# Layer norm, attention and SwiGLU on one core: row 0's mean from two scaled sums, its statistics behind row 1's

## The chip, the cores and the metric

The kernel runs on one core of one Trainium2 chip. The metric is the device time of one execution in microseconds; the time given is the median of several. Lower is better.

## The reference

```python
def reference(A_x, A_wqkv, A_wo, B_x, B_w_gate, B_w_up, B_w_down):
    x  = A_x                                  # 1 x 2048 x 576, bf16
    xn = _layernorm(x)                        # (x - mean) / sqrt(var + 1e-5)
    # A: 32 heads of 18, each token sees itself and 7 tokens at steps of 2 behind it
    q, k, v = split(xn @ wqkv)
    logits = q . k[pos - 2*w] * 18**-0.5, w = 0..7   # masked to -1e9 where pos - 2*w < 0
    o = softmax(logits) . v[pos - 2*w]
    # B: SwiGLU with 4608 hidden columns
    return x + o @ wo + (silu(xn @ w_gate) * (xn @ w_up)) @ w_down
```

Bodies are shortened here; all inputs are bf16 and drawn as normal values times 0.05.

## The kernel before

The 2048 tokens are cut into 16 rows of 128 tokens: partition p holds tokens 16p to 16p+15, and row r is the r-th token of every partition. A row's work is then 128 partitions by 576 columns. The kernel runs in two stages.

**QKV stage, the first 60 us.** Rows of x are loaded (row 0 through ACT's queue, rows 1 to 3 one by one and the rest in three blocks of four through SP's). For each row DVE takes the statistics (`ln_stats`: `bn_stats` on each half of the columns in `ln_half`, then `bn_aggr` in `ln_aggr`), ACT the square root of the variance (`ln_sqrt`), DVE its reciprocal (`ln_recip`) and the normalized row (`ln_apply`). The normalized row is 576 columns and a copy of its last 64, 640 in all, so that the contraction makes four slabs (kt) of 128 and a fifth, kt=4, of twice the same 64. The row is transposed into `xnT`: rows 1 to 4 on TensorE (`transp_pe` for row 1, `transp_halves` for rows 2 to 4, with copies out of PSUM by ACT and DVE), rows 5 and on by a transposing DMA (`transp_dma`). Then TensorE multiplies it with wqkv in four groups g of 432 columns (`p_mm`, L301), and `p_evac` takes the sums out of PSUM.

Row 0 differs. Its QKV product is taken from the centered row alone: `ln_center` (L251) subtracts the mean, `ln_center_pad` does it for the last 64 columns on GpSimd, TensorE transposes it, the copies go to `xcT` instead of `xnT`, and `p_evac(0, ...)` multiplies with 1/std while it takes the sums out (L365, L367). Since the second stage wants the normalized row 0 in `xnT` too, `ln_apply(0)` makes it in `xn0` (in the space of the later tile A) and `transp_dma(0)` turns it.

Row 0 multiplies with whole 128-row slabs for kt 0 to 3 (`p_whole`). Its kt=4 (`p_row0_rest`) and all of the later rows use two 64-row halves that run beside each other (`p_row`). Where the two halves exchange their banks a GpSimd no-op stands between them as a fence (`fence_after`, `fence_before`, L314): the matmul behind it waits for GpSimd's queue to come to that point.

PSUM has 8 buffers, taken in turn: the warm-up's (also `pt1`), `pa` and `pb` for transposes, `t` for row 0's four groups, `u` for row 1's.

**The second stage** runs over four blocks of 512 tokens. For each it multiplies `xnT` with w_gate and w_up (L600), takes silu and the product (L611 to L613), and multiplies the result with w_down and the attention's output with wo (L629). The attention itself is DVE work that is interleaved there (`chain`).

The order of the work is written out by hand: `manual_schedule` keeps each engine's instructions in the order of the calls. Every engine runs its queue in that order, so the calls on lines 477 to 550 are the order on each engine. SP's queue issues nearly all transfers, and a transfer that waits for its data holds up those behind it. The start, before:

```python
    warm_pe(10, 1)
    ln_open(0)
    ln_stats(0)
    ln_center_pad(0)
    ln_center(0, 0, P)
    ln_sqrt(0)
```

The functions that the diff touches, and what calls them:

Of the kernel before, what the change touches and what calls it, by code (L numbers as in the profile page):

```python
# [10 lines left out]
f32 = mybir.dt.float32  # L11
ACT = mybir.ActivationFunctionType
ALU = mybir.AluOpType
# [4 lines left out]
P = 128  # L18
H, DH, W, DIL = 32, 18, 8, 2
D = H * DH  # L20
HALF = D // 2
# [4 lines left out]
DPAD = KT * P  # L26
# [44 lines left out]
def kernel(  # L71
# [11 lines left out]
    nc = tc.nc  # L83
# [9 lines left out]
    const = ctx.enter_context(tc.tile_pool(name="const", bufs=1))  # L93
# [19 lines left out]
    PP = big.tile([P, 2, RT * D], bf16, name="PP")  # L113
# [65 lines left out]
    def load_gu(it):  # L179
        ch, slot = it % NCH, it % NSLOT  # L180
        fc = slice(ch * FC * P, (ch + 1) * FC * P)
        nc.sync.dma_start(gu[:, slot, 0:4, :], B_w_gate[0:512, fc].rearrange("(kt kp) n -> kp kt n", kp=P))
        nc.sync.dma_start(gu[:, slot, 4:8, :], B_w_up[0:512, fc].rearrange("(kt kp) n -> kp kt n", kp=P))
        nc.sync.dma_start(gu[0:64, slot, 8, :], B_w_gate[512:576, fc])
        nc.sync.dma_start(gu[64:128, slot, 8, :], B_w_up[512:576, fc])
# [10 lines left out]
    def new_ps(name):  # L196
        return ps.tile([P, 512], f32, name=name, tag="ps")


    ln = {}  # L200

    def ln_open(c):
        mv = lns.tile([P, 4, 2], f32, name="mv")
        rstd = lns.tile([P, 4], f32, name="rstd")
        ln[c] = (xc_b[c], xn_b[c % 2], mv, rstd)

    sums = {}

    def ln_half(r, k):
        c, j = divmod(r, 4)  # L210
        xc, xn, mv, rstd = ln[c]
        if k == 0:
            sums[r] = lns.tile([P, 2, 6], f32, name="stats")
        nc.vector.bn_stats(sums[r][:, k, :], xc[:, j, k * HALF:(k + 1) * HALF])  # L214

    def ln_aggr(r):
        c, j = divmod(r, 4)
        nc.vector.bn_aggr(ln[c][2][:, j, :], sums[r][:].rearrange("p c s -> p (c s)"))

    def ln_stats(r, n=1):  # L220
        for i in range(r, r + n):
            ln_half(i, 0)
            ln_half(i, 1)
            ln_aggr(i)

    def ln_sqrt(r, n=1):
        c, j = divmod(r, 4)
        xc, xn, mv, rstd = ln[c]
        nc.scalar.activation(rstd[:, j:j + n], mv[:, j:j + n, 1], ACT.Sqrt, bias=eps_t[:], scale=1.0)

    def ln_recip(r, n=1):
        c, j = divmod(r, 4)
        rstd = ln[c][3]
        nc.vector.reciprocal(rstd[:, j:j + n], rstd[:, j:j + n])

    def ln_apply(r):
        c, j = divmod(r, 4)
        xc, xn, mv, rstd = ln[c]
        dst = xn[:, j] if r else xn0
        nc.vector.tensor_scalar(dst[:, 0:D], xc[:, j], mv[:, j, 0:1], rstd[:, j:j + 1],  # L240
                                op0=ALU.subtract, op1=ALU.mult)
        if r < 2:
            nc.gpsimd.tensor_scalar(dst[:, D:DPAD], xc[:, j, 512:D], mv[:, j, 0:1], rstd[:, j:j + 1],
                                    op0=ALU.subtract, op1=ALU.mult)
        else:
            nc.vector.tensor_copy(dst[:, D:DPAD], dst[:, 512:D])

    def ln_center(r, lo=0, hi=D):
        c, j = divmod(r, 4)
        xc, xn, mv, rstd = ln[c]  # L250
        nc.vector.tensor_scalar(xn[:, j, lo:hi], xc[:, j, lo:hi], mv[:, j, 0:1], None, op0=ALU.subtract)  # L251

    def ln_center_pad(r):
        c, j = divmod(r, 4)
        xc, xn, mv, rstd = ln[c]
        nc.gpsimd.tensor_scalar(xn[:, j, D:DPAD], xc[:, j, 512:D], mv[:, j, 0:1], None, op0=ALU.subtract)

    def transp_pe(r, kts, pt):
        c, j = divmod(r, 4)
        xn = ln[c][1]  # L260
        for i, kt in enumerate(kts):
            nc.tensor.transpose(pt[:, i * P:(i + 1) * P], xn[:, j, kt * P:(kt + 1) * P], ident[:])  # L262

    def xT_of(r):
        return xcT if r == 0 else xnT[:, :, r * P:(r + 1) * P]

    def copy_pt(eng, r, kts, pt):
        eng(xT_of(r)[:, kts[0]:kts[-1] + 1, :],
            pt[:, 0:len(kts) * P].rearrange("p (k t) -> p k t", t=P))

    def new_pt():
        return ps.tile([P, 8 * P], bf16, name="pt", tag="ps")
# [16 lines left out]
    def transp_dma(r):  # L289
        c, j = divmod(r, 4)  # L290
        nc.sync.dma_start_transpose(xnT[:, :, r * P:(r + 1) * P], ln[c][1][:, j, :] if r else xn0)
# [7 lines left out]
    def p_mm(t, g, kt, half, r, start, stop):  # L299
        rows = slice(0, P) if half is None else slice(64 * half, 64 * half + 64)  # L300
        return nc.tensor.matmul(t[g][:, 0:G], xT_of(r)[rows, kt, :], w_at(g, kt, rows),  # L301
                                start=start, stop=stop)

    def p_whole(r, t, kt, gs=range(NG)):
        for g in gs:
            p_mm(t, g, kt, None, r, kt == 0, False)
# [14 lines left out]
    def p_row(r, between=None, at=(0, 1), t=None):  # L321


        done = t is not None
        t = t or [None] * NG
        fence = {}
        for swap in range(2):
            for i in range(2):
                for kt in (0, 1, 2, 3) if swap else (0, 4, 1, 2, 3):
                    if done and kt == 0:  # L330
                        continue
                    for half in range(2):
                        g = i + 2 * (half ^ swap)
                        if t[g] is None:
                            t[g] = new_ps("qkv_ps")
                        mm = p_mm(t, g, kt, half, r, swap == 0 and kt == 0, swap == 1 and kt == 3)
                        if swap == 0 and kt == 3 and half == 1:
                            fence[i] = fence_after(mm)
                        if swap and kt == (1 if done else 0) and half == 0:
                            fence_before(mm, fence[i])  # L340
                    if swap and (i, kt) == at and between is not None:
                        between()
        return t

    def p_evac(r, t, only=range(6), between=None, last=6, dve=(5,)):


        c, j = divmod(r, 4)
        ks, vs = stage[2 * c % 4], stage[(2 * c + 1) % 4]
        vdst = vs[:, j, :].rearrange("p (d h) -> p d h", h=H)  # L350
        parts = [
            (QO[:, r, 0:G], t[0][:, 0:G]),
            (ks[:, j, HALF:D], t[2][:, 0:HALF]),
            (vdst[:, :, 0:8], t[2][:, HALF:G].rearrange("p (h d) -> p d h", d=DH)),
            (QO[:, r, G:D], t[1][:, 0:D - G]),
            (ks[:, j, 0:HALF], t[1][:, D - G:G]),
            (vdst[:, :, 8:H], t[3][:, 0:G].rearrange("p (h d) -> p d h", d=DH)),
        ]
        for n in only:
            if n == last:  # L360
                between()
            if r:
                (nc.vector.tensor_copy if n in dve else nc.scalar.copy)(*parts[n])  # L363
            elif n in dve:
                nc.vector.tensor_scalar(*parts[n], ln[0][3][:, 0:1], None, op0=ALU.mult)  # L365
            else:
                nc.scalar.mul(*parts[n], ln[0][3][:, 0:1])  # L367
# [99 lines left out]
    def normalize(r, n=1):  # L467
        ln_recip(r, n)
        for i in range(r, r + n):
            ln_apply(i)  # L470
            if i > 4:
                transp_dma(i)
# [3 lines left out]

    warm_pe(10, 1)
    ln_open(0)
    ln_stats(0)
    ln_center_pad(0)  # L480
    ln_center(0, 0, P)
    ln_sqrt(0)
    pa, pb = new_pt(), new_pt()
    transp_pe(0, (0,), pa)
    ln_center(0, P, D)
# [3 lines left out]
    ln_stats(1)  # L489
    ln_sqrt(1)  # L490
    copy_pt(nc.scalar.copy, 0, (3, 4), pb[:, 2 * P:])
    ln_recip(0)
    ln_apply(0)
    ln_recip(1)
    ln_apply(1)

    t = [new_ps("qkv_ps") for g in range(NG)]
    p_whole(0, t, 0)
    p_whole(0, t, 1)
    p_whole(0, t, 2, (0, 1))  # L500
    transp_pe(1, (0, 1), pt1)
    transp_pe(1, (2,), pa)
    copy_pt(nc.scalar.copy, 1, (0, 1), pt1)
    copy_pt(nc.vector.tensor_copy, 1, (2,), pa)
    p_whole(0, t, 2, (2, 3))
    transp_pe(1, (3, 4), pb)
    copy_pt(nc.scalar.copy, 1, (3, 4), pb)
    u = [None] * NG
    for g in (0, 2, 1, 3):
        u[g] = new_ps("qkv_ps")  # L510
# [2 lines left out]
    p_row0_rest(t)  # L513
    ln_stats(2)
    ln_sqrt(2)
    normalize(2)
    p_evac(0, t, (5, 0, 3, 2, 4, 1), dve=(5, 2))
    ln_half(3, 0)
    ln_half(3, 1)
    load_gu(0)  # L520
    transp_dma(0)

    p_row(1, turn(2), (0, 1), u)
    ln_aggr(3)
# [3 lines left out]
    normalize(3)  # L528
    ln_open(1)
    ln_stats(4)  # L530
    for ring in (Kr, Vr):
        nc.sync.dma_start(ring[0:1, 0:HALO, :], wz[0:1, :].unsqueeze(1).to_broadcast([1, HALO, D]))

    t = p_row(2, turn(3))
    ln_stats(5)
# [5 lines left out]
    t = p_row(3, turn(4))  # L541
# [10 lines left out]
    for r in range(4, R):  # L552
        t = p_row(r)
# [92 lines left out]
    for tt in range(NTT):  # L646
# [28 lines left out]
        for sub in range(0, RT, 2):  # L675
            t, fence = {}, {}
# [36 lines left out]
```

## Time and profile before

| | |
|---|---|
| median of 3 runs | 503.44 us (503.23 to 503.55) |
| the profiled execution | 503.32 us, of which the span of the profile is 501.5 |
| TensorE matmuls | 496.8 us busy, 99% of the span |
| VectorE (DVE) | 329.0 us, 66% |
| ScalarE (ACT) | 200.6 us, 40% |
| GpSimd (POOL) | 2.6 us, 1% |
| row 0 of x landed, first BN_STATS | 3.78 us |
| first QKV matmul | 6.01 us |
| first matmul of the second stage | 59.66 us |

In the profile each row of a time line gives the start in us, the duration, the engine, the line of the kernel and the operation with what it writes and reads; in brackets stand the idle time of the engine just before it and what ended it. PEld is TensorE's weight load, which overlaps the matmuls before it. ACTq and SPq are the sequencers that issue transfers. Matmul ends are modelled, so it is their starts that are compared. A chain line gives start, duration and what the end of the kernel was waiting on in that time.

### The profile page before, as it was taken

How to read it: one execution, taken by the hardware profiler on the slowest of the kernel's cores; microseconds unless marked ns; L12 is line 12 of the kernel's file. 1: busy time of each engine (PE TensorE's matmuls, PEld its weight loads, DVE VectorE, ACT ScalarE, POOL GpSimd, SP SyncE). 2: the span in 40 equal slices, each digit the busy share in tenths (PEclk: the TensorE clock that was granted, in tenths of full speed). 3: DMA queues.
4: the chain of work that ended last, by engine and by line, in shares of the span. 5: the costliest groups of instructions: out<-in, count | busy, mean ns of one | idle time of the engine just before them, and what ended most of it. 6: DMA issues, size and time to landing. Idle time of an engine off the chain costs nothing.

```text
span 501.5 us, 13267 instructions
## 1 busy us (share of the span) xinstructions
PE 496.8 (99%) x5795; PEld 282.8 (56%) x5795; DVE 329.0 (66%) x478; ACT 200.6 (40%) x415; POOL 2.6 (1%) x9
## 2 busy tenths in 40 slices
PE   8999999999999999999999999999999999999997
PEld 4555544444677644444777544445777444446775
DVE  5889597998999698999897139995980222221001
ACT  4756657645300255544300445557000454553000
POOL 2000000000000000000000000000000000000000
PEclk9999999999999999999999999999999999999999
DMA  8689989898731045535631154453700335442200
GB/s 322 164 207 228 320 268 294 260 318 272 186 114 61 25 147 185 190 112 174 166 106 47 30 182 154 131 189 110 181 26 14 106 110 177 159 126 39 76 14 25
DMA packets 77186, 75.42 MB, mean 150 GB/s; under 512 B 22708, under 2 KB 72528, under 8 KB 77128
## 3 DMA queue, kind: packets, MB, share of 16 engines
q1 hardware_dynamic: 76840, 73.98, 49.2%
q8 instruction: 45, 0.74, 0.7%
q10 hardware_dynamic: 288, 0.59, 0.3%
q14 instruction: 13, 0.11, 0.1%
HBM read 58.76 MB, written 5.90 MB: 129 GB/s over the span
## 4 chain that ended last, share of the span: by engine, by line
PE 98%; DMA 1%; DVE 0%; SPq 0%; issue 0%
PE g_ps L600 56%; PE d_ps L629 32%; PE qkv_ps L301 11%; DMA hT<-in_A_wqkv_dram 1%; DVE ot L643 0%; PE pt L283 0%; SPq L145 0%; PE pt L262 0%; PE warm_ps L262 0%
## 5 line engine op out<-in xcount | busy, mean ns | idle before, releaser
L600 PE MATMUL g_ps<-xnT,gu 64*128 64x512 bf16 x2592 | 280.4, 376 | 0.0
L600 PEld LDWEIGHTS <-gu 64*128 64x128 bf16 x2592 | 126.1, 94 | 152.9
L611 ACT ACTIVATE sg<-g_ps 128x512 bf16<-128x512 f32 x144 | 87.3, 606 | 156.6 <-PE g_ps L600 156.6
L629 PE MATMUL d_ps<-wd,hT 64*128 64x288 bf16 x2304 | 146.4, 283 | 0.0
L629 PEld LDWEIGHTS <-hT 64*128 64x128 bf16 x2304 | 112.2, 94 | 29.7
L613 DVE TENSOR_TENSOR hT<-sg,uc 128x512 bf16<-128x512 bf16 x144 | 60.0, 419 | 93.9 <-ACT uc L612 93.8
L612 ACT CAST uc<-g_ps 128x512 bf16<-128x512 f32 x144 | 85.2, 592 | 0.0
L414 DVE TENSOR_REDUCE PP<-PP 128x64 f32<-128x1152 bf16 x64 | 84.9, 1346 | 0.4
L301 PE MATMUL qkv_ps<-hT,xnT 64*128 64x432 bf16 (+1 forms) x536 | 50.1, 343 | 0.0
L409 DVE TENSOR_TENSOR PP<-QO,Kr 128x2304 bf16<-128x2304 bf16 (+1 forms) x35 | 43.5, 1249 | 7.0 <-DMA Kr<-hT 6.8
L641 DVE TENSOR_TENSOR ot<-d_ps,xr 128x288 bf16<-128x288 f32 x30 | 12.3, 450 | 51.1 <-PE d_ps L629 51.1
L441 DVE TENSOR_TENSOR PP<-Vr,A 128x2304 bf16<-128x2304 bf16 (+1 forms) x35 | 43.2, 1250 | 0.4
L301 PEld LDWEIGHTS <-xnT 64*128 64x128 bf16 (+1 forms) x536 | 25.9, 94 | 22.5 <-ACT xnT L287 0.2
L446 DVE TENSOR_TENSOR PP<-PP 128x2304 bf16<-128x2304 bf16 x24 | 32.5, 1353 | 0.3
L611 ACT ACT_TABLE_LOAD x5 | 6.4, 1283 | 47.2 <-PE g_ps L600 47.2
L629 PE MATMUL d_ps<-wo,xnT 64*128 64x288 bf16 x288 | 22.9, 283 | 0.0
L363 ACT CAST hT<-qkv_ps 128x288 bf16<-128x288 f32 (+2 forms) x58 | 21.1, 427 | 0.5 <-ACT hT L363 0.5
L434 ACT ACTIVATE PP<-PP 128x1024 f32<-128x1024 f32 x4 | 4.2, 1056 | 31.2 <-DVE PP L430 31.2
L629 PEld LDWEIGHTS <-xnT 64*128 64x128 bf16 x288 | 14.0, 94 | 3.6
L643 ACT CAST ot<-d_ps 128x288 bf16<-128x288 f32 x1 | 0.4, 399 | 38.8 <-PE d_ps L629 38.8
L363 ACT CAST QO<-qkv_ps 128x432 bf16<-128x432 f32 (+1 forms) x30 | 12.3, 409 | 7.4 <-PE qkv_ps L301 7.4
L214 DVE BATCH_NORM_STATS2 stats<-wd 128x6 f32<-128x288 bf16 x32 | 12.9, 444 | 2.8 <-DMA wd<-in_A_x_dram 2.6
(53 smaller groups left out, 89.4 us busy)
## 6 DMA issues: line engine op xcount, KB each, us to landing
gu<-in_B_w_gate_dram SPq DMA_DIRECT2D x36, 512.0 KB, 3.9
gu<-in_B_w_up_dram SPq DMA_DIRECT2D x36, 512.0 KB, 5.2
wd<-in_B_w_down_dram SPq DMA_DIRECT2D x9, 576.0 KB, 6.4
kv_d<-hT SPq DMA_DIRECT2D x5, 576.0 KB, 6.0
gu<-in_B_w_gate_dram SPq DMA_DIRECT2D x36, 64.0 KB, 5.0
gu<-in_B_w_up_dram SPq DMA_DIRECT2D x36, 64.0 KB, 4.6
xr<-in_A_x_dram SPq DMA_DIRECT2D x8, 288.0 KB, 3.9
out_dram<-ot SPq DMA_DIRECT2D x16, 144.0 KB, 1.8
```

The lines of the kernel that those rows point to most:

```text
L214: nc.vector.bn_stats(sums[r][:, k, :], xc[:, j, k * HALF:(k + 1) * HALF])
L301: return nc.tensor.matmul(t[g][:, 0:G], xT_of(r)[rows, kt, :], w_at(g, kt, rows), start=start, stop=stop)
L363: (nc.vector.tensor_copy if n in dve else nc.scalar.copy)(*parts[n])
L409: nc.vector.tensor_tensor(prod[:, a:b], QO[:, RT * tt + a:RT * tt + b, :], Kr[:, s:s + b - a, :], op=ALU.mult)
L414: nc.vector.tensor_reduce(L[:, w, rs], prod[:, rs].rearrange("p r (h d) -> p r h d", d=DH), axis=AX.X, op=ALU.add)
L441: nc.vector.tensor_tensor(dst[:, a:b], Vr[:, s:s + b - a, :].rearrange("p r (d h) -> p r d h", h=H), A[:, w, a:b].unsqueeze(2).to_broadcas ...
L446: nc.vector.tensor_tensor(dst, acc, pv, op=ALU.add)
L600: mm = nc.tensor.matmul(ring_ps[j][b][:], gu[rows, slot, k, fc], xnT[rows, kt, tok], start=(swap == 0 and kt == 0), stop=(swap == 1 and kt ...
L611: nc.scalar.activation(sg[:], t[0][:], ACT.Silu)
L612: nc.scalar.copy(uc[:], t[1][:])
L613: nc.vector.tensor_tensor(hT[:, ch * FC + j, :], sg[:], uc[:], op=ALU.mult)
L629: mm = nc.tensor.matmul(t[sub][h][:, 0:HALF], a[rows], w[rows, h * HALF:(h + 1) * HALF], start=(swap == 0 and n == 0), stop=(swap == 1 and ...
```

## The change

Row 0's mean no longer comes from `bn_stats` and `bn_aggr`. A new function `ln_mean0` sums each half of the columns, scaled by 1/576: the first half by an ACT activation with an accumulator output, the second by a DVE tensor_scalar with one. The two parts stand in a new tile `part`, and `ln_center` and `ln_center_pad` subtract both in one instruction (the diff of the pad, on GpSimd, is the same as that of `ln_center`). The scaled elements themselves go to a part of PP that nothing reads.

Row 0's statistics are still needed for 1/std. They are taken behind row 1's: the first half while row 1 waits for its square root, the second half and the aggregate behind row 1's normalization. Row 0's square root comes behind row 1's copies out of PSUM, its reciprocal behind row 2's statistics. Row 1's transposes stand one matmul earlier among row 0's kt=2 groups, and the copy of its third block goes from DVE to ACT. `ln_apply(0)` goes behind row 4's statistics, and `transp_dma(0)` behind the two writes of the halo's zeros on SP.

```diff
+    part = const.tile([P, 2], f32, name="part")
+    def ln_mean0():
+        xc = ln[0][0]
+        nc.scalar.activation(PP[:, 1, 0:HALF], xc[:, 0, 0:HALF], ACT.Copy, scale=1.0 / D, accum_out=part[:, 0:1])
+        nc.vector.tensor_scalar(PP[:, 1, HALF:D], xc[:, 0, HALF:D], 1.0 / D, None,
+                                op0=ALU.mult, op1=ALU.add, accum_out=part[:, 1:2])
...
     def ln_center(r, lo=0, hi=D):
...
-        nc.vector.tensor_scalar(xn[:, j, lo:hi], xc[:, j, lo:hi], mv[:, j, 0:1], None, op0=ALU.subtract)
+        nc.vector.tensor_scalar(xn[:, j, lo:hi], xc[:, j, lo:hi], part[:, 0:1], part[:, 1:2],
+                                op0=ALU.subtract, op1=ALU.subtract)
...
     ln_open(0)
-    ln_stats(0)
+    ln_mean0()
     ln_center_pad(0)
     ln_center(0, 0, P)
-    ln_sqrt(0)
     pa, pb = new_pt(), new_pt()
...
     ln_stats(1)
     ln_sqrt(1)
     copy_pt(nc.scalar.copy, 0, (3, 4), pb[:, 2 * P:])
-    ln_recip(0)
-    ln_apply(0)
+    ln_half(0, 0)
     ln_recip(1)
     ln_apply(1)
+    ln_half(0, 1)
+    ln_aggr(0)
...
     p_whole(0, t, 1)
-    p_whole(0, t, 2, (0, 1))
+    p_whole(0, t, 2, (0,))
     transp_pe(1, (0, 1), pt1)
     transp_pe(1, (2,), pa)
     copy_pt(nc.scalar.copy, 1, (0, 1), pt1)
-    copy_pt(nc.vector.tensor_copy, 1, (2,), pa)
-    p_whole(0, t, 2, (2, 3))
+    p_whole(0, t, 2, (1, 2))
     transp_pe(1, (3, 4), pb)
+    copy_pt(nc.scalar.copy, 1, (2,), pa)
     copy_pt(nc.scalar.copy, 1, (3, 4), pb)
+    p_whole(0, t, 2, (3,))
+    ln_sqrt(0)
...
     ln_stats(2)
     ln_sqrt(2)
+    ln_recip(0)
     normalize(2)
...
     load_gu(0)
-    transp_dma(0)
...
     ln_stats(4)
+    ln_apply(0)
     for ring in (Kr, Vr):
         nc.sync.dma_start(ring[0:1, 0:HALO, :], wz[0:1, :].unsqueeze(1).to_broadcast([1, HALO, D]))
+    transp_dma(0)
```

More of the change, by code (lines that the diff above doesn't have):

```diff
@@ L255, in ln_center_pad @@
         xc, xn, mv, rstd = ln[c]
-        nc.gpsimd.tensor_scalar(xn[:, j, D:DPAD], xc[:, j, 512:D], mv[:, j, 0:1], None, op0=ALU.subtract)
+        nc.gpsimd.tensor_scalar(xn[:, j, D:DPAD], xc[:, j, 512:D], part[:, 0:1], part[:, 1:2],
+                                op0=ALU.subtract, op1=ALU.subtract)
     def transp_pe(r, kts, pt):
```

## The prediction

> **What bounds the kernel now.** I read the share of each engine first, then the chain that ended last over the first 15 us, then the time line of the start, and last the single rows of TensorE (starts to the nanosecond, rounded here to 0.01 or 0.001 us).
>
> The page and the chain:
> ```profile
> PE 496.8 (99%) x5795; PEld 282.8 (56%) x5795; DVE 329.0 (66%) x478; ACT 200.6 (40%) x415; POOL 2.6 (1%) x9
> ...
> PE 98%; DMA 1%; DVE 0%; SPq 0%; issue 0%
> ...
> 1.17 4.79 DMA hT<-in_A_wqkv_dram
> 5.97 0.04 issue
> 6.01 1.99 PE qkv_ps L301 x10
> 8.00 0.11 PE warm_ps L262 x2
> 8.11 0.06 PE pt L262
> 8.16 0.36 PE qkv_ps L301 x2
> 8.53 0.11 PE pt L262 x2
> 8.64 3.68 PE qkv_ps L301 x30
> ```
> From 6.01 us on the end is set by TensorE alone, and before that by a transfer: the first slab of wqkv (kt=0, the first L149 of SP), issued at 1.17 and landed at 5.97. Taking the starts of TensorE's rows one by one, a 432-column matmul follows the one before it every 0.1825 us and a transpose every 0.056 us; from 6.01 to the last matmul at 498.1 only two places lose more than 0.03 us against that step: 0.10 us ahead of row 1's first matmul (8.57), and 0.10 us at row 0's 64-row halves (10.14). So all that any edit at the start can give behind 6.01 is 0.2 us, and what precedes 6.01 hangs on the transfer.
>
> The time line shows row 0's statistics and the first of the two losses:
> ```profile
> 3.78 0.82 DVE L214 BATCH_NORM_STATS2 stats<-wd 128x6 f32<-128x288 bf16 x2 [2.60 <-DMA wd<-in_A_x_dram]
> 4.63 0.21 DVE L218 BATCH_NORM_AGGREGATE mv<-stats 128x2 f32<-128x12 f32 x1
> 4.88 0.56 DVE L251 TENSOR_SCALAR wd<-wd,mv 128x128 bf16<-128x128 bf16 x2
> 5.45 0.27 ACT L268 COPY PP<-pt 128x128 bf16<-128x128 bf16 x1 [0.28 <-PE pt L262]
> 7.01 0.43 DVE L240 TENSOR_SCALAR wd<-wd,mv,rstd 128x576 bf16<-128x576 bf16 x1
> 8.14 0.37 ACT L268 COPY xnT<-warm_ps 128x256 bf16<-128x256 bf16 x1 [1.14 <-PE warm_ps L262]
> ```
> Row 0's centering starts 4.88; its first transposed block is copied by 5.72 and its weight load runs at 5.77, yet the matmul starts at 6.01, 0.04 behind the landing. Row 0's statistics are thus 0.2 us off the path already. Row 1's copy out of PSUM ends at 8.51, and the weight load that needs it runs at 8.57: that is the first loss.
>
> **The mean (removed: two BN_STATS, one aggregate; added: one accumulating instruction on ACT, one on DVE).** Removed from 3.78 to 4.84. No row of this trace writes a sum beside its output. DVE's half: nearest is BN_STATS on the same 288 elements, 0.45. ACT's half: between a CAST of 288 elements (0.40) and an ACTIVATE of 288 with a pointer scale (0.50); reading the sum out I bound by nothing and by the smallest ACT instruction of the start (0.20) or the square root (0.29). So 0.40 to 0.80; I take 0.60 (0.40+0.20), as the scale is a constant. Both start at 3.78 (one transfer releases them); centering starts at 3.78+0.60+0.04 = 4.42, bounds 4.22 to 4.62, against 4.88.
> By the Trainium skill ("VectorE: DVE Perf Modes", § Two Vector instructions with no wait between them) an op that writes out its accumulator is two instructions, the main one and an accumulator read; "ScalarE: Activation LUTs" (§ What ACT_TABLE_LOAD costs) gives an ACTIVATE with constant scale 186 ns + 0.833 ns an element, 0.43 us for 288 by estimate, ahead of that read. By the two the mean is not the single step that the source shows, and the sum would be the same. No row of before shows either.
>
> **What the earlier centering is worth: nothing.** The chain centering, transpose, copy, weight load is 0.89 us long (4.88 to 5.77), so row 0's first block is ready at 5.31 instead of 5.77, and the matmul waits on to 5.97 for the transfer, which is issued by SP before any of this. First matmul 6.01, as before. Centering with two scalars instead of one: the 576-element apply with two scalars takes 0.43, the 448-element centering with one 0.40, so nothing for it. POOL's pad (0.58, to about 5.1) frees the fifth transpose before the later blocks are due at 6.7.
>
> **Row 1 first, row 0's statistics behind.** From centering to the end of row 1's apply is 2.57 us (4.88 to 7.44); the first half of row 0's BN_STATS (0.45) lies in the wait for row 1's square root, where L234 and L240 of row 0 lay (6.33 to 6.82). Row 1 is ready at 4.42+2.57 = 6.99. Its transposes now stand one matmul earlier, their weight load due at 7.47, not 7.65: slack 0.48. POOL works on row 1's pad at once instead of behind row 0's (0.74).
>
> **The gain.** The sequence g0, transposes 0-2, g1, g2, transposes 3-4, g3 holds the same 4 matmuls and 5 transposes. Transposes 0-2 start at 7.65 instead of 7.83, so ACT's copy runs 7.96 to 8.33 and row 1's weight load could run at 8.38; TensorE reaches row 1's first matmul at 7.468 + 4x0.1825 + 5x0.056 = 8.48. The wait is gone with 0.09 to spare, against a loss of 0.105 now (row 1's second matmul starts 8.765, due 8.659). The third copy goes from DVE to ACT: 8.24 to 8.51, needed 8.84; the last 8.50 to 8.87, needed 9.03. What is late next is nothing: kt=3 lands 8.84, needed 9.21; kt=4 lands 9.58, needed 10.04. The second 0.10 us stays: its transfers have landed 0.56 earlier, and the row grouping changes from 128 to 64 there in both orders.
>
> **The rest, all beside TensorE.** Row 0's square root and reciprocal: aggregate done near 7.4, ACT free at 8.87, reciprocal near 9.2; row 0's evacuation needs it at 10.43. Row 2's apply ends near 9.9 (10.38 now); its transposes are due at 11.9. ln_apply(0) on DVE behind row 4's statistics: 0.43 into an idle 0.33 before L287 at 15.78; at most 0.1 late, and the next deadline there, row 4's transposes at 18.65, has 0.2 of slack. Its POOL pad stands between row 1's second fence (12.20) and row 2's first (14.36) and waits only for the reciprocal of 9.2: 0.74 us, over by 13, 1.4 us ahead of that fence. On SP, the two halo writes go ahead and transp_dma(0) then holds SP from 11.3 or so to 17.3 instead of to 12.8; queued behind it is row 5's transposing DMA, not issued before 19.03 anyway. Row 0's xnT is first read at 59.66. Cost nothing; if one of these covers failed it would be the fence, in the Pool queue, with TensorE behind it.
>
> Sum: 0 - 0.105 = **-0.10 us** on the profiled execution (span 501.5, 503.32 in all, 0.12 under the median of 503.44). So 503.22 against that one, 503.34 against the median; forecast **503.3**.
>
> **Rivals.**
> *No gain:* ACT's copy comes later than I place it by more than the 0.09 spare, or the first matmul's landing moves by a tenth. Against it: the copy's releaser moves 0.18 by the order alone. It gives 503.44.
> *The mean is late (slower):* it decides once centering starts after 4.90 for row 1 (7.47 less 2.57) or 5.07 for row 0 (5.95 less 0.89), that is at 1.1 us for the accumulating pair. At twice my upper bound (1.6) centering starts at 5.42, the first matmul at 6.35 (+0.34), and row 1's transposes wait to 8.03 for 7.81 (+0.22): 0.56 - 0.10 = +0.46, 503.8. For more than 1 us it would take 2.2 us. Against it: no DVE or ACT instruction of the start exceeds 0.67 but the table load.
> *The clock falls back (slower):* the start shows a slow phase, warm-up matmuls every 0.427 us until about 3.3 and 0.219 after. The transposes move to about 4.7, leaving TensorE quiet from about 5.3 to 6.01 in place of 4.53 to 5.18. If that brought the slow phase back for as long as it lasted at first (2.9 us), half of it is lost: 1.45 us, 504.8. For: transposes may not keep it up. Against: the quiet before them was as long (0.66) and the next matmuls ran at full step.
> The Trainium skill ("TensorE: Matmul & The Clock Gate", Part 1 and Part 4) has the clock halved after an idle window of about 3.4 us and transposes not counted as busy; by that rule 1.48 us without a matmul (4.53 to 6.01) stays too short in both kernels, and the trace of before agrees (0.1825 a matmul at once).
>
> **How the numbers follow.** Forecast 0.70, no gain 0.20, late mean 0.07, clock 0.03. A measurement of this kernel tells about 0.2% (1 us) from no change; the first three stay within it but for a tail. Faster by more than that: 0.01, as only 0.2 us of stalls exist. Slower: 0.03 for the clock and 0.02 of the late mean. Same: 0.94. The range takes the runs' own scatter (0.2 either way) around 503.2 and reaches to the late mean: 503.0 to 503.8.
>
> **What would show it.** Right: first matmul still at 6.01 behind the landing, centering near 4.4, row 1's first matmul near 8.48 without a wait, everything behind shifted by 0.1, the 0.10 at the halves kept. Wrong: a wait on DVE or ACT ahead of the first matmul, a step of 0.36 behind it, a Pool wait in row 2, or row 5 waiting for its DMA.

## The result and the profile after: slower by 0.14%

The changed kernel takes 504.05 us (median of 22 runs) against 503.28 for the kernel before (22 runs beside it): ratio 1.0014, 95% interval 1.0008 to 1.0021. One of the changed kernel's 22 runs took 581.83 us at a granted clock of 0.851; it counts in the median and not in the ratio. The change is 0.4 to 1.1 us slower, by its ratio within the 0.2% that the prediction called no change, but outside its range (503.0 to 503.8) and on the other side of its forecast. The profiled execution took 503.84 us, its span 502.1.

The first line of the page after, and the chain of the changed kernel's start, where the before chain had its transfer to 5.97 and its first matmul at 6.01:
```profile
span 502.1 us, 13273 instructions
...
1.19 4.51 DMA hT<-in_A_wqkv_dram
5.70 0.04 issue
5.74 1.80 PE qkv_ps L310 x9
7.54 0.11 PE warm_ps L271 x2
7.66 0.06 PE pt L271
7.71 0.36 PE qkv_ps L310 x2
8.08 0.11 PE pt L271 x2
8.19 3.81 PE qkv_ps L310 x31
```
The start is not slower but faster: the first matmul still stands 0.04 us behind the landing of the first slab of wqkv, which came 0.27 earlier in this execution, and row 1's matmuls follow its transposes with no 0.10 us of waiting. (Half of that is lost again at 8.98, of which more below.) TensorE's last matmul starts at 497.78, against 498.10 before. Yet the span is 0.5 us longer: from that start to the end it is 4.28 us, against 3.43 before. So the loss lies behind the last matmul, where the prediction had not looked.

The new instructions in the time line (start, duration, engine, line):
```profile
3.89 0.44 ACT L212 ACTIVATE PP<-wd 128x288 bf16<-128x288 bf16 x1 [0.74 <-DMA wd<-in_A_x_dram]
3.90 0.45 DVE L213 TENSOR_SCALAR_CACHE_REDUCE PP<-wd 128x288 bf16<-128x288 bf16 x1 [2.69 <-DMA wd<-in_A_x_dram]
...
4.24 0.19 ACT L212 ACTIVATION_READ_ACCUMULATOR PP<-wd 128x1 f32 x1
4.27 0.08 DVE L213 DVE_READ_ACCUMULATOR PP<-wd 128x1 f32 x1
...
4.47 0.62 DVE L258 TENSOR_SCALAR wd<-wd,part 128x128 bf16<-128x128 bf16 x2
```
Each half of the mean is two entries in its engine's queue. Centering starts 0.58 us behind the sums (forecast 0.64).

The end, in the view of transfers from just before the last output's issue to the end; first before, then after. The last line is that output with its time from issue to landing:
```profile
DMA packets 144, 0.15 MB, mean 55 GB/s; under 512 B 16, under 2 KB 144, under 8 KB 144
...
out_dram<-ot SPq DMA_DIRECT2D x1, 144.0 KB, 1.7
```
```profile
DMA packets 145, 0.16 MB, mean 52 GB/s; under 512 B 16, under 2 KB 144, under 8 KB 144
...
q14 instruction: 1, 0.01, 1.5%
...
out_dram<-ot SPq DMA_DIRECT2D x1, 144.0 KB, 2.6
```
Here is the difference: one packet of the kind "instruction", 8 KB, that before does not have in this stretch, and an output that takes 0.9 us longer to land. By the single packets the 8 KB run from 499.56 to 500.27; 15 of the output's 16 landing marks come by 500.35, the last at 501.21. That last one belongs to eight packets of 1152 bytes and a closing one of 4 bytes: the first of them starts at 500.27, just when the 8 KB packet ends, and the last at 500.71, while all the others of the output have ended by 499.99. The trace does not name a packet's engine, but by these times one of the 16 DMA engines did the fetch first and its share of the output after. Before, the same packet starts at 502.56, behind the end of the span.

Whose fetch it is shows in the counts. ACT's entries in the trace (compute, and the semaphore waits and drains between, which compute nothing, all in order) are 574 before and 578 after: the accumulating activation and its read, a wait and the copy that came from DVE. Before, packets of 8 KB on that queue fall where ACT stands at its 192nd, 320th and 448th entry (103.77, 223.88, 345.74 us), 128 entries apart, so the next is due near the 576th. The queue carries other packets too, which do not go by ACT's count: with eight more entries on ACT, in an experiment below, these three come 4.5 to 7.4 us earlier (99.25, 217.05, 338.31), while the others behind 60 us move by less than 0.4 (107.09 and 106.97, 462.06 and 462.18). Before, ACT ends with 574. After, its 574th entry is the last copy out of PSUM (498.12), the 575th the drain behind it.

### The profile page after: what moved, and what is told of

It is laid out like the page before. It is cut to its first block, busy times and chain, and to the rows that moved or that the text cites. A ratio compares the mean times of both kernels' runs of the same rounds, so it can differ in the third digit from the quotient of the medians.

```text
span 502.1 us, 13273 instructions
## 1 busy us (share of the span) xinstructions
PE 496.7 (99%) x5795; PEld 321.5 (64%) x5795; DVE 329.3 (66%) x479; ACT 201.1 (40%) x418; POOL 2.7 (1%) x9
## 4 chain that ended last, share of the span: by engine, by line
PE 98%; DMA 1%; DVE 0%; SPq 0%; issue 0%
PE g_ps L613 56%; PE d_ps L642 32%; PE qkv_ps L310 11%; DMA hT<-in_A_wqkv_dram 1%; DVE ot L656 0%; PE pt L292 0%; SPq L145 0%; PE pt L271 0%; PE warm_ps L271 0%
## 5 line engine op out<-in xcount | busy, mean ns | idle before, releaser
L613 PEld LDWEIGHTS <-gu 64*128 64x128 bf16 x2592 | 143.7, 94 | 135.4
L642 PEld LDWEIGHTS <-hT 64*128 64x128 bf16 x2304 | 127.7, 94 | 14.2
L310 PEld LDWEIGHTS <-xnT 64*128 64x128 bf16 (+1 forms) x536 | 29.6, 94 | 18.9 <-ACT xnT L296 0.2
L642 PEld LDWEIGHTS <-xnT 64*128 64x128 bf16 x288 | 16.0, 94 | 1.7
```

The source lines that it names most:

```text
L613: mm = nc.tensor.matmul(ring_ps[j][b][:], gu[rows, slot, k, fc], xnT[rows, kt, tok], start=(swap == 0 and kt == 0), stop=(swap == 1 and kt ...
L642: mm = nc.tensor.matmul(t[sub][h][:, 0:HALF], a[rows], w[rows, h * HALF:(h + 1) * HALF], start=(swap == 0 and n == 0), stop=(swap == 1 and ...
```

## The experiments

Theory F: the changed kernel is slower because ACT's queue has four entries more, which moves the fetch of its next block onto the last output transfer. Rival S: something at the start or in the body costs. Rival D: the gain of the start is not real. Idle copies of one element on ACT in the second stage change the count; in the traces they stand between 76 and 100 us (not at 66 to 90, as the texts of the expectations have it) and take 0.17 to 0.28 us each. (The ratios are not the quotients of the two medians, from which they differ by up to 0.0003.)
```diff
+    fill = const.tile([P, n], f32, name="fill")
...
+            if tt == 0 and 1 <= ch <= (n + 1) // 2:
+                for i in range(2 * ch - 2, min(2 * ch, n)):
+                    nc.scalar.copy(fill[:, i:i + 1], eps_t[:])
```

**The changed kernel with four of them** (n = 4).

> The changed kernel with four one-element ACT copies more, in idle ACT time of the second stage (66 to 90 us). Theory F (a fetch of ACT's instructions, 8 KB, meets the last output transfer because ACT's queue has 4 more entries than before): with 4 more still, the 576th entry is passed well before the last output, the fetch falls near 460 to 480 us, the last transfer lands 1.7 us after its issue instead of 2.6, and the time is about 503.2, 0.8 below the changed kernel and 0.1 below the kernel before. Theory S (the moved work costs at the start or in the body): the copies change nothing of it, 504.0.

503.00 (11 runs; before 503.37; ratio 0.9993, 0.9984 to 1.0002). With more work on ACT the kernel is 1.05 us faster than the changed one, as F says, and no run of the one reaches the other's range (502.87 to 503.31 against 503.84 and more). From the view of transfers at the end, no instruction packet is left:
```profile
DMA packets 144, 0.15 MB, mean 51 GB/s; under 512 B 16, under 2 KB 144, under 8 KB 144
...
out_dram<-ot SPq DMA_DIRECT2D x1, 144.0 KB, 1.7
```

**The kernel before with four.**

> The kernel before with the same four idle ACT copies, so that ACT's queue has about as many entries as in the changed kernel. Theory F: the fetch moves from behind the end (502.6) to about 500, beside the last output transfer, which then lands 2.6 us after its issue; 504.0 to 504.2, slower by 0.7 to 0.9. Theory S: 503.3, no change.

504.16 (before 503.37; 1.0014, 1.0005 to 1.0023): a loss of 0.79 us, without any part of the change. With the run above, S falls. Of the profiled execution's loss, 0.54 lies behind the last matmul (3.97 us to the end against 3.43); another 0.14 lies ahead of it, between the first and the last matmul (492.23 against 492.09), and F does not explain that part. The same view has the fetch again:
```profile
DMA packets 145, 0.16 MB, mean 56 GB/s; under 512 B 16, under 2 KB 144, under 8 KB 144
...
q14 instruction: 1, 0.01, 1.2%
...
out_dram<-ot SPq DMA_DIRECT2D x1, 144.0 KB, 2.4
```

**The kernel before with eight.**

> The kernel before with eight such copies. Theory F: the fetch falls near 460 to 480 us, last transfer 1.7 us from issue to landing, 503.3 as before, though it has twice the added work of the kernel with four. If the copies themselves cost (theory C), it is slower than with four: by F's rival it would be about 504.8 if four give 504.1.

503.31 (before 503.37; 0.9999, 0.9990 to 1.0008): twice the copies cost nothing, so the copies themselves are not what four cost.

**The copy of row 1's third block back on DVE** in the changed kernel.
```diff
-    copy_pt(nc.scalar.copy, 1, (2,), pa)
+    copy_pt(nc.vector.tensor_copy, 1, (2,), pa)
```

> The changed kernel with the copy of row 1's third block back on DVE, one ACT entry less. Theory F: the entry whose passing starts the fetch moves by one, from the last copy or the drain behind it to the drain or the wait for the other engines; if to the latter, the fetch is behind the end and the time is 503.2; if still to the drain, 504.0. Either way the time is one of these two and nothing between. Theory S, with that copy as the cost: between 503.3 and 503.9, by what the copy costs at the start.

503.36 (before 503.37; 1.0000, 0.9991 to 1.0009). The fetch is behind the end (502.05) and the output lands in 1.74 us, but the time is not the 503.2 expected. The trace has the missing part: ACT's 576th entry, now a drain at the end, starts 0.38 us behind the 575th, where the same two entries are 0.09 apart before. The step at the block's edge is 0.29 longer. Of this 0.17 reaches the end (from the last matmul 3.60 us, against 3.43), as the entry behind it follows after 0.28 instead of 0.40. The 8 KB packet starts only 0.92 behind the 576th entry, so this is not a wait for that packet; what it is stays open.

**The kernel before with three**, to see that cost alone.

> The kernel before with three idle ACT copies: the last copy of ACT is then its 573rd entry of the trace, as in the changed kernel with the copy on DVE. Theory F with the 575th entry as the trigger: the fetch starts behind the last output's landing, near 502, so the transfer is not met (1.7 us from issue to landing), but ACT's 576th entry, a drain at the end, waits for it by about 0.3; 503.6 to 503.7. If the trigger were the 574th, the drain behind the copy: 504.1, as with four copies. If only the start mattered: 503.4.

503.50 (before 503.25; 1.0003, 0.9994 to 1.0012): 0.25 above, as expected in size, though the interval does not part it from none. In its trace the 575th entry is at 500.99, the 576th at 501.35, against 0.09 apart before, and the fetch packet at 502.24; the end comes 0.17 later (501.70 against 501.53), with the last matmul at 498.10 in both. In the kernel before with eight copies the 576th entry is one of three semaphore waits at 476 us, and it stands 0.33 behind the 575th there too, against 0.05 between the same two waits before; there nothing waits for it.

**The kernel before with six, and with five.**

> The kernel before with six idle ACT copies: the last copy is then ACT's 576th entry. Theory F: the entries 573 to 575 are passed near 476 us, so the fetch falls near 477 and the end is not met: 503.3, where four copies gave 504.2. Theory C (each added copy costs): above 504.2.

503.25 (before 503.25; 0.9998, 0.9989 to 1.0007), fetch at 477.15. As expected.

> The kernel before with five idle ACT copies: the last copy is ACT's 575th entry. Theory F: the fetch follows the 575th entry by about 1.0 us, so it starts near 499.9, beside the last output transfer as with four copies: 504.0 to 504.2, while six give 503.25. If the reach of the effect is one count alone, 503.3.

503.42 (before 503.24; 1.0004, 0.9995 to 1.0013), output landed in 1.73 us. Theory F as I had put it was wrong here: the last copy is the 575th entry and runs at 498.68, but the fetch came at 477.45. A copy that waits for its data seems to be passed by the sequencer ahead of its run, while a drain or a semaphore wait holds it. So of the counts that ran only one hits the output: the one at which the drain behind the last copy is the 575th entry, which is where the change put it.

**The order of TensorE's work alone** on the kernel before, with seven idle copies.
```diff
-    p_whole(0, t, 2, (0, 1))
+    p_whole(0, t, 2, (0,))
...
-    copy_pt(nc.vector.tensor_copy, 1, (2,), pa)
-    p_whole(0, t, 2, (2, 3))
+    p_whole(0, t, 2, (1, 2))
     transp_pe(1, (3, 4), pb)
+    copy_pt(nc.scalar.copy, 1, (2,), pa)
     copy_pt(nc.scalar.copy, 1, (3, 4), pb)
+    p_whole(0, t, 2, (3,))
```

> The kernel before with one part of the change alone: row 1's transposes one matmul earlier and the copy of its third block on ACT; row 0's mean, statistics, normalization and turning DMA as before. Seven idle ACT copies more put the fetch of ACT's instructions well before the end, as in the kernels with 8. Theory P (the prediction's sum is right for what TensorE sees): the 0.10 us wait ahead of row 1's first matmul is gone, 503.2 to 503.3, 0.1 below the kernel before with eight copies. Theory X (the gain of 0.37 that the changed kernel with 4 copies shows comes from earlier centering, the first matmul being bound by the later of the transfer and row 0's block): the same 0.1 here, and the rest in the other part.

503.23 (before 503.25; 0.9998, 0.9989 to 1.0007): the 0.1 is not there. In the time line of weight loads row 1's transposes now wait for its normalization:
```profile
7.59 0.17 PEld L262 LDWEIGHTS <-wd 128*128 128x128 bf16 x3 [0.33 <-DVE wd L240]
```
TensorE loses 0.07 us there, so most of the wait that the order removes comes back as another: the order needs the earlier row 1. A further 0.05 is lost ahead of 9.21, where row 0's kt=3 matmuls wait for their slab of wqkv, which landed at 9.17 in this execution (8.84 before).

**The mean and the moved statistics alone**, with TensorE's order as before and six idle copies. The edit is the last diff turned round, on the changed kernel.

> The changed kernel with the order of TensorE's work and the copies of row 1 as before (third block on DVE), and six idle ACT copies more, so that the fetch falls well before the end: the mean from two sums, the moved statistics, normalization and turning DMA alone. Theory P: no gain at the start, as the transfer sets the first matmul; but row 1 is ready earlier and still waits for ACT's copy, 503.3 to 503.4. Theory X: 0.2 to 0.3 below the kernel before, 503.1.

503.17 (before 503.25; 0.9997, 0.9988 to 1.0006): 0.08 below, between the two theories and not to be parted from either. In its profiled execution the first matmul, at 5.80, stood 0.04 behind the transfer (5.76), as Theory P has it; but TensorE was still in its slow phase, with row 0's transposes 0.107 us apart, and the first two steps of the matmuls took 0.31 and 0.26 for 0.18. The wait ahead of row 1's first matmul is still there, as forecast.

**The changed kernel with two idle copies**, taken as the fewest that move the fetch away. (By the kernel before with five, one might do; that was not run.)

> The changed kernel with two idle ACT copies, the fewest that should carry the last copy to the 576th entry. Theory F: fetch near 477, last transfer 1.7 us, and the whole gain of the start is left, 503.0 to 503.1 (0.2 to 0.35 below the kernel before). If the gain with four copies was scatter: 503.3.

503.00 (before 503.24; 0.9998, 0.9989 to 1.0007), fetch at 476.79, output landed in 1.73 us. It is the version to keep of these: its median lies 0.24 below the kernel before (by the ratio 0.10), that with four copies 0.37 (0.35), and neither interval excludes no gain.

All counts together; "landing" is the last output's time from issue to landing in the profiled execution:

| kernel | last copy is ACT's entry | fetch packet, us | landing, us | median, us | before beside it |
|---|---|---|---|---|---|
| before | 570 | 502.56 | 1.74 | 503.28 | |
| before + 3 | 573 | 502.24 | 1.74 | 503.50 | 503.25 |
| changed, copy on DVE | 573 | 502.05 | 1.74 | 503.36 | 503.37 |
| before + 4 | 574 | 500.05 | 2.38 | 504.16 | 503.37 |
| changed | 574 | 499.56 | 2.60 | 504.05 | 503.28 |
| before + 5 | 575 | 477.45 | 1.73 | 503.42 | 503.24 |
| before + 6 | 576 | 477.15 | 1.74 | 503.25 | 503.25 |
| changed + 2 | 576 | 476.79 | 1.73 | 503.00 | 503.24 |
| before + 8 | 578 | 477.09 | 1.73 | 503.31 | 503.37 |
| changed + 4 | 578 | 476.98 | 1.73 | 503.00 | 503.37 |
| before, order alone, + 7 | 578 | 476.97 | 1.74 | 503.23 | 503.25 |
| changed, old order, + 6 | 579 | 458.68 | 1.74 | 503.17 | 503.25 |

## Why the prediction was wrong

**The mean: right.** 0.58 us to centering, where it took 0.64 from 0.60 and 0.04. Its rivals of a late mean and a fall of the clock behind earlier transposes did not happen; the matmuls behind 5.74 run at full step. Subtracting two scalars was not free, though: the two pieces of the centering took 0.62 us where they had taken 0.56, so that from centering to row 0's weight load it is 0.95 us, not 0.89. It cost nothing, as the transfer came later still.

**"What the earlier centering is worth: nothing": true of the execution it was read from, not of all.** Of the seven traces with the old start, three (before, and before with three and with four copies) have the first matmul at 6.01, just behind the transfer, which landed at 5.97. In the four others the transfer landed at 5.74 to 5.80 and the matmul came later than 0.04 behind it. In the kernel before with six copies it had landed at 5.77, x's row 0 came later (its statistics begin at 3.94, not 3.78), and the chain runs from that:
```profile
0.71 3.21 DMA wd<-in_A_x_dram
3.92 0.02 issue
3.94 0.83 DVE stats L214 x2
4.77 0.02 issue
4.80 0.22 DVE mv L218
5.02 0.02 issue
5.04 0.57 DVE wd L251 x2
```
and in the time line of weight loads:
```profile
5.94 0.30 PEld L301 LDWEIGHTS <-PP 128*128 128x128 bf16 x3
```
The first matmul came at 5.94, behind row 0's weight load, where 5.81 would have been 0.04 behind the transfer: 0.13 for the earlier centering to win. In the order alone (5.87, transfer 5.80) and with eight copies (5.87, transfer 5.78) it is 0.03 to 0.05; with five (6.01, transfer 5.74) TensorE's slow phase had a part in it. With the new start the first matmul stands 0.04 or 0.05 behind the transfer in all five traces: 5.74 in the changed kernel, 6.04 with four copies, 5.86 with the copy on DVE, 5.66 with two copies, 5.80 with the old order. So the prediction's reading of the transfer holds for the kernel after; for the kernel before, one profile of a race between two transfers had been taken for the rule.

**The gain at row 1: right in the whole change.** From first to last matmul the changed kernel with four copies takes 491.99 us and the kernel before 492.09: the 0.105 of the sum. With two copies and in the changed kernel itself it is 492.04. The changed kernel loses 0.05 at 8.98, where a matmul waits for the kt=3 slab of wqkv, landed at 8.94: with all of the start 0.27 earlier, that slab was late, where "What is late next is nothing" had counted on a first matmul at 6.01. With the third block's copy back on DVE it is 492.00, so the gain did not need that copy on ACT. The second 0.10, at the 64-row halves, stayed in every trace.

**The rest, beside TensorE: right** in what it named. GpSimd's pad ran at 11.94 and was over 1.5 us ahead of row 2's fence; no wait of TensorE shows there, and none for row 5.

**The step that failed** is the sum itself: it ended at the last matmul and took what lies behind it (3.4 us) as fixed, and it counted an instruction only by its duration. "The third copy goes from DVE to ACT" was costed by ACT's times alone, at nothing; with the accumulator's read, the activation and a wait it was also four entries in ACT's queue, and that term, 0.8 to 1.05 us, was missing: 504.16 less 503.37 on the kernel before, 504.05 less 503.00 on the changed one. The landing of the last output accounts for 0.86 of it in the changed kernel's trace (2.60 less 1.74) and for 0.64 in that of the kernel before with four copies (2.38 less 1.74). With the 0.86 the sum would have been -0.10 + 0.86 = +0.76, against +0.77 between the medians; that it fits so well is in part luck, as the gain at the start differs between executions. The page before held the hint in its list of queues (packets and MB within the span):
```profile
q8 instruction: 45, 0.74, 0.7%
...
q14 instruction: 13, 0.11, 0.1%
```
The second line has ACT's fetches among others; the single packets show the next one at 502.56, 1.0 us behind the end. That a few entries more would bring it onto the output could not be read from the page alone.

The Trainium skill ("Runtime: NRT & Kernel Launch", § Instruction fetch mechanics) has an engine's sequencer fetch its instructions by a DMA queue of its own, in blocks of 16 KiB, and calls the crossing of a block mostly hidden. The traces agree that instructions come by DMA queues apart from the data (q8 and q14 above), but q14 serves more than ACT. They differ on the size (8 KB, 128 entries, for ACT here), and at the end of the kernel the crossing was not hidden: 0.27 to 0.29 us at the edge, 0.17 of it at the end, and 0.64 to 0.86 where the fetch met the last transfer.

What stays open: how much the start gains over many executions. The ratios say 0.10 and 0.35, the traces 0.05 to 0.10 at row 1 and from nothing to 0.13 at the first matmul, and the intervals reach to nothing. Open too is how far ahead of its work ACT's sequencer runs, which decides the exact count that hits.

## What to carry to other kernels

The end of a kernel belongs to the sum: from the last compute instruction to the end count the last transfer, and see whether an instruction packet starts beside it or shortly behind the end, as a few entries more or less on one engine can move it there. A loss of under 1 us that no engine's rows explain is tested by adding idle instructions: if the time falls again with more of them, the cause is where the entries lie in the queue and not what they do. A start that hangs on two transfers issued at once is a race; one profile shows one of its outcomes.

## What the runs showed of the hardware that was not expected

- A fetch of 8 KB of instructions beside the last output took 0.71 us (0.55 in the kernel before with four copies), and eight of the output's 128 packets of 1152 bytes started only when it had ended (500.27; 500.60 with four copies on the kernel before).
- The loss is not monotone in the number of instructions: 0, 3, 4, 5, 6 and 8 idle copies on the kernel before give 503.28, 503.50, 504.16, 503.42, 503.25 and 503.31 us, beside 503.24 to 503.37 for that kernel without them.
- TensorE's slow phase did not end at one time: before, matmuls went at full step from 3.65 us; in the kernel before with five copies row 0's transposes were still 0.107 us apart at 5.9 and the first QKV matmul took 0.36 for 0.18.
